# Chains of a Fourier filter and soft mixture of experts: two batches in one stationary operand, row steps behind the chain's copies, three weight loads under way

## The chip, the core and the metric

The kernel runs on one core of one Trainium2 chip. The metric is the device time of one execution in microseconds (us). The kernel has TensorE (PE; its weight loads are shown as PEld), VectorE (DVE), ScalarE (ACT), GpSimd (POOL), the SyncE queue (SP) that issues nearly all DMAs, and 16 DMA engines.

## What is computed

x has 8 batches of 2496 tokens and 256 features. Each feature is filtered along the tokens by a product in the frequency domain, and the result, as 19968 tokens, goes through a soft mixture of 8 experts with 4 slots each.

```python
X = np.fft.rfft(x, axis=1)
y = np.fft.irfft(X * (filt_r + 1j * filt_i)[None], n=2496, axis=1)
x = y.reshape(19968, 256)
logits = x @ phi                        # 32 slots
d = softmax(logits, axis=0)             # over all tokens: dispatch
slot_in = (d.T @ x).reshape(8, 4, 256)
slot_out[e] = relu(slot_in[e] @ w1[e]) @ w2[e]      # w1 256x1024, w2 1024x256
c = softmax(logits, axis=1)             # over the slots of each token: combine
out = c @ slot_out
```

All is float32; one matrix product of float32 is two loads and two passes on TensorE, a transposition one of each.

## The kernel before

2496 = 39 x 64, and the Fourier transform is done in two steps by matrix products. The first step (`s1_unit`, tile s) multiplies the 39-point part, its result `at` goes to DRAM (a_dram) and comes back turned (ash). `x_unit` does the 64-point part (tile x) and multiplies with the filter on DVE (tiles t, yt; from batch 6 on partly on POOL), in ten units of two rows for each batch. `t_unit` transposes the result (tile t on TensorE, y in SBUF) and makes logits in the frequency domain (tile l, lt). The filtered tokens themselves are never formed: the mixture works on y and on logits that a small inverse transform makes.

This second part is a chain for each group of batches: groups 0, 1 and 2 are pairs, (0,1), (2,3), (4,5), and groups 3 and 4 are the single batches 6 and 7. The chain (function `chain`, a generator) goes through transposed logits (ltr, copied to lsb by DVE), two steps of an inverse transform (v1 products into v_0, v_7 and v_14, by the first of their seven rows, copied by ACT; transposed; lg products), the running maximum (cm, cmax, mt, mx, mb, m_run), the exponential of the dispatch (d, by DVE and ACT), the forward transform of it (u products, copied to u by ACT; transposed and copied to u2 by DVE; dd products, copied by ACT), sums z and s with y, and then the row steps (`rows`) for the softmax over slots: maximum rm, difference and exponential in place in lg, sum r_all, reciprocal. For groups 0 and 1 the finished lg is written to DRAM (c_dram) and read back at the end (cl).

In the products v1 and u the stationary operand is 32 slots of one batch wide. A pair makes four products, which write the four strips of 32 partitions of PSUM, for batch and half. A single batch makes two.

The order of instructions on each engine comes from a scheduler that follows data dependences and the order of the program text; `behind` and `not_before` add a dependence of order alone, with no wait on a semaphore. In the program, each slot of the main loop (80 slots, ten for each batch) issues an x unit, one or two first steps, a t unit and two hops of the active chain, where a hop runs to the next `yield`. The last two chains are interleaved by the table `TAIL`, and there `in_line` makes TensorE keep the program's order. The expert weights, 64 blocks of 256 KB in the order `WORDER`, are loaded by SP into buffers as they come free (`load_w`, `load_ws`): the filter table ff_t, then ash, t2, yb, y and yt in the first 43, and y again for the rest, as s of the last batches releases them. A load waits for the buffer, and SP goes strictly in order. Then come the expert layers (h, ht, o, slot_out), and the combine with the output (ct, out, ob), which SP writes to DRAM.

## Time and profile before

| | |
|---|---|
| runs | 396.33, 396.37, 392.46 us; median 396.33 |
| profiled execution | 398.42 us, span of its instructions 396.6 us, mean granted TensorE clock 0.924 |
| TensorE busy | 359.1 us of products, 267.3 us of weight loads |
| DVE, ACT, POOL busy | 257.5, 177.0, 151.7 us |
| DMA | 103.99 MB, mean 262 GB/s |
| first output issued | 343.47 us from the span's start |

Times in the profile count from the span's start. Matrix products overlap, so their busy time isn't a rate; the rate of a run of products is read from its length in the chain of waits, divided by their number. The granted clock is the share of full speed at which TensorE ran. In the DMA view, queue q1 holds the kernel's own transfers, and the queues marked "instruction" bring instructions to the engines. What lies between the span and the execution's time is 1.8 us.

### The profile page before, as it was taken

The numbers are of one execution on the slowest core, as the hardware profiler recorded it, in microseconds if no ns is written. First come the engines' busy times: TensorE is split into PE (matmuls) and PEld (weight loads), VectorE is DVE, ScalarE is ACT, GpSimd is POOL, SyncE is SP. The second block draws the span as 40 slices with busy tenths as digits, with TensorE's granted clock in tenths as the row PEclk, the third lists the DMA queues.
The fourth block names the chain that finished last, engine by engine and source line by source line (L and its number), as shares of the span: only waits on it lengthen the run. The fifth ranks groups of instructions, "written<-read, shape, count | busy, mean of one in ns | idle before, by whom it ended". The sixth has DMA issues, their size and how long they took to land.

```text
span 396.6 us, 11597 instructions
## 1 busy us (share of the span) xinstructions
PE 359.1 (91%) x4778; PEld 267.3 (67%) x4778; DVE 257.5 (65%) x517; ACT 177.0 (45%) x357; POOL 151.7 (38%) x182
## 2 busy tenths in 40 slices
PE   8998798869998999999799999998988899999970
PEld 6985476647765766765576678787667544778970
DVE  1484767763899966589986555897553453586650
ACT  2554344525456533545734354463352431575540
POOL 0374645526545243255515284553221131361000
PEclk9999989987999999999989999999995999996555
DMA  8769999898889896868867576773488597299997
GB/s 316 257 213 301 289 272 311 287 333 241 283 279 322 240 285 209 264 196 267 251 206 224 170 208 187 271 215 106 135 266 319 193 250 252 114 415 415 417 417 294
DMA packets 50155, 103.99 MB, mean 262 GB/s; under 512 B 5218, under 2 KB 23394, under 8 KB 47926
## 3 DMA queue, kind: packets, MB, share of 16 engines
q1 hardware_dynamic: 49412, 102.83, 78.2%
q8 instruction: 38, 0.62, 0.6%
q10 hardware_dynamic: 690, 0.42, 0.4%
q14 instruction: 15, 0.12, 0.1%
HBM read 63.11 MB, written 40.12 MB: 260 GB/s over the span
## 4 chain that ended last, share of the span: by engine, by line
PE 72%; DVE 9%; DMA 9%; POOL 3%; issue 3%; ACT 2%; SPq 0%; POOLq 0%; DVEq 0%; ACTq 0%
PE x L423 14%; PE t L452 7%; PE out L1054 7%; PE s L355 7%; DMA xt<-in_x 5%; PE s L496 5%; PE l L470 4%; PE v L496 4%; DMA ash<-a_dram 3%; PE dd L496 3%; PE lg L496 3%; PE u L496 2%; PE s L396 2%; PE h L998 2%; PE o L1016 2%
## 5 line engine op out<-in xcount | busy, mean ns | idle before, releaser
L423 PE MATMUL x<-cst_t,ash 128*128 128x128 f32 x640 | 91.2, 285 | 5.3 <-DMA ash<-a_dram 2.9
L423 PEld LDWEIGHTS x<-cst_t,ash 128*128 128x128 f32 x640 | 81.3, 196 | 16.0 <-DVE t L440 5.3
L334 POOL TENSOR_TENSOR eo<-xt 128x512 f32<-128x512 f32 (+1 forms) x40 | 48.5, 1212 | 104.6 <-issue 61.0
L440 DVE TENSOR_TENSOR t<-x,ff_t 128x512 f32<-128x512 f32 x80 | 54.9, 686 | 49.6 <-PE x L423 33.0
L364 ACT COPY at<-s 128x1024 f32<-128x1024 f32 (+1 forms) x42 | 39.5, 941 | 58.0 <-PE s L355 37.8
L452 PE MATMUL t<-cst_t,yt 128*128 128x128 f32 x320 | 52.8, 285 | 0.0
L452 PEld LDWEIGHTS t<-cst_t,yt 128*128 128x128 f32 x320 | 37.0, 144 | 20.4 <-issue 11.1
L337 POOL TENSOR_TENSOR eo<-xt 128x512 f32<-128x512 f32 (+1 forms) x40 | 49.6, 1239 | 0.0
L355 PE MATMUL s<-eo,w1q_t 64*64 64x512 f32 (+1 forms) x336 | 43.9, 593 | 5.4 <-POOL eo L337 5.4
L460 ACT COPY y<-t 128x512 f32<-128x512 f32 x58 | 33.5, 589 | 21.1 <-PE t L452 18.1
L442 DVE TENSOR_TENSOR x<-x,ff_t 128x512 f32<-128x512 f32 x60 | 41.6, 695 | 1.3
L1054 PE MATMUL out<-so,st 32*128 32x256 f32 x468 | 35.9, 367 | 1.0 <-DVE ob L1059 0.8
L1054 PEld LDWEIGHTS out<-so,st 32*128 32x128 f32 x468 | 32.8, 252 | 3.4 <-DVE ob L1059 1.4
L1059 DVE COPY ob<-out 128x512 f32<-128x512 f32 (+1 forms) x40 | 25.2, 670 | 8.4 <-PE out L1054 7.5
L443 DVE TENSOR_TENSOR yt<-x,t 128x256 f32<-128x256 f32 x60 | 25.1, 418 | 7.7 <-PE l L470 6.4
L470 PE MATMUL l<-yt,phi_t 128*32 128x128 f32 x640 | 27.5, 286 | 2.6 <-ACT y L460 2.0
L1059 ACT COPY ob<-out 128x512 f32<-128x512 f32 (+1 forms) x40 | 21.9, 581 | 14.0 <-PE out L1054 11.5
L443 POOL TENSOR_TENSOR yt<-yt,t 128x256 f32<-128x256 f32 x20 | 15.0, 750 | 33.1 <-DVE yt L442 33.1
L470 PEld LDWEIGHTS l<-yt,phi_t 128*32 128x32 f32 x640 | 16.0, 111 | 13.8 <-issue 7.5
L480 ACT COPY lt<-l 128x128 f32<-128x128 f32 x40 | 10.6, 266 | 33.0 <-PE l L470 32.8
L444 DVE TENSOR_TENSOR yt<-x,t 128x256 f32<-128x256 f32 x60 | 24.7, 412 | 0.0
L496 PE MATMUL u<-cst_t,d 117*32 117x60 f32 (+1 forms) x704 | 15.3, 219 | 5.3 <-ACT u L634 2.7
(116 smaller groups left out, 505.1 us busy)
## 6 DMA issues: line engine op xcount, KB each, us to landing
xt<-in_x SPq DMA_DIRECT2D x35, 512.0 KB, 5.6
ash<-a_dram SPq DMA_DIRECT2D x70, 256.0 KB, 4.0
out<-ob SPq DMA_DIRECT2D x17, 1024.0 KB, 8.0
a_dram<-at SPq DMA_DIRECT2D x56, 240.0 KB, 4.6
w<-in_wx SPq DMA_DIRECT2D x32, 256.0 KB, 4.1
w<-in_wx SPq DMA_DIRECT2D x6, 512.0 KB, 5.1
x_t<-in_x SPq DMA_DIRECT2D x5, 512.0 KB, 5.5
ff_t<-in_ff SPq DMA_DIRECT2D x10, 256.0 KB, 5.4
```

What stands on the lines that cost most here:

```text
L334: ins = eng.tensor_tensor(out=eo[:, 0, 0:n], in0=xs[:, :, 0], in1=xs[:, :, 1], op=ALU.add)
L337: ins = eng.tensor_tensor(out=eo[:, 1, 0:n], in0=xs[:, :, 0], in1=xs[:, :, 1], op=ALU.subtract)
L355: ins = pe.matmul(ps, w1q_t[q, c], eo[q, c, 0:n], start=True, stop=True)
L423: ins = pe.matmul(ps[:, 2 * k + dh].rearrange("q r c -> q (r c)"), ash[:, k, dh * P : (dh + 1) * P], C("a1" if t0 + k else "b0"), start=Tr ...
L440: dve.tensor_tensor(out=t2, in0=ps[:, :, ::-1, :], in1=fiv, op=ALU.mult)
L442: dve.tensor_tensor(out=part, in0=ps, in1=frv, op=ALU.mult)
L443: add.tensor_tensor(out=yt[:, :, 1, :], in0=part[:, :, 1, :], in1=t2[:, :, 1, :], op=ALU.add)
L452: pe.transpose(pt[:, k, dh, :], yt[:, c % 2, 2 * k + dh].rearrange("q r c -> q (r c)"), ident)
L470: ins = pe.matmul(pl[32 * j : 32 * j + 32, :], phi_t[:, dh, :], yt[:, j // 2, 2 * (j % 2) + dh].rearrange("q r c -> q (r c)"), start=(dh = ...
L496: line(pe.matmul(*a, **k))
L1054: nc.tensor.matmul(prs[k][:, mm, :], sts[n][q, hs, c0 : c0 + P], so[q, ho], start=(i == 0), stop=(i == 2))
L1059: copy(ob[:, nm * k : nm * (k + 1), :], prs[k])
```

## The change

- Pairs: lsb, d, u2, dd, lg and cl are laid out with the two batches of a pair side by side, so that one product takes 64 columns (both batches) as its stationary operand. v1 and u make two products where there were four. For single batches (M = 32) nothing changes.
- Row steps: in groups 0 to 2 the first row step on DVE (maximum) is ordered behind the last copy of u2 on DVE, and the exponentials on ACT behind the last copy of dd on ACT. This is an order of issue, not a wait on a semaphore.
- Weight loads: for the loads from ash to yt (`calm`), each load waits until the load three places before it in the program has landed. The loads before and after it have no such wait.

```diff
--- before.py
+++ after.py
@@ -72,6 +72,7 @@
 WL = 4
 SB = 3
 AT_ONCE = 1
+UNDER_WAY = 3


 def slot_of(b, u):
@@ -509,16 +510,17 @@

         nb = len(bs)
         R = nb * 64
-        lsb = wk.tile([P, nb, NT, SLOTS], F32, tag="cc", name=f"lsb_{g}", bufs=1)
+        M = nb * SLOTS
+        lsb = wk.tile([P, NT, nb, SLOTS], F32, tag="cc", name=f"lsb_{g}", bufs=1)

         def ltr(b2, i0):
             b = bs[b2]
-            lf = lsb[:, b2].rearrange("k t e -> k (t e)")
             pl = psum([P, 4, P], f"ltr_{b}_{i0}")
             n = min(4, 5 - i0)
             for i in range(n):
                 pe_t(pl[:, i, :], lts[b][:, i0 + i, :], ident)
-            dve.tensor_copy(lf[:, i0 * P : (i0 + n) * P], pl.rearrange("k i q -> k (i q)")[:, 0 : n * P])
+            lf = pl.rearrange("k i (j e) -> k (i j) e", j=4)
+            dve.tensor_copy(lsb[:, 4 * i0 : 4 * (i0 + n), b2], lf[:, 0 : 4 * n])

         for b2 in range(nb):
             for i0 in (0, 4) if nb == 2 else (0,):
@@ -532,22 +534,20 @@
             n = min(7, NT - t0)
             pv = psum([P, 7, KP // 2, 2], f"v1_{g}_{t0}")
             for t in range(t0, t0 + n):
-                for b2 in range(nb):
-                    for h in range(2):
-                        q = (b2 * 2 + h) * 32
-                        pe_m(
-                            pv[q : q + 32, t - t0].rearrange("q k r -> q (k r)"),
-                            lsb[:, b2, t, :],
-                            C("m1" if t else "m0", h * KP, (h + 1) * KP),
-                            start=True,
-                            stop=True,
-                        )
+                for h in range(2):
+                    pe_m(
+                        pv[M * h : M * h + M, t - t0].rearrange("q k r -> q (k r)"),
+                        lsb[:, t].rearrange("k b e -> k (b e)"),
+                        C("m1" if t else "m0", h * KP, (h + 1) * KP),
+                        start=True,
+                        stop=True,
+                    )
             act.copy(v1[0:R, :, :, t0 : t0 + n], pv[0:R, 0:n].rearrange("q t k r -> q k r t"))
             yield f"v1_{t0}"
         v = wk.tile([QP, NH, R], F32, tag="cb", name=f"v_{g}", bufs=1)
-        lg_t = lgp.tile([KR, NH, nb, 2, SLOTS], F32, tag=f"lg{max(g, NSPILL)}", name=f"lg_{g}")
+        lg_t = lgp.tile([KR, NH, 2, nb, SLOTS], F32, tag=f"lg{max(g, NSPILL)}", name=f"lg_{g}")
         lgs[g] = lg_t
-        lg = lg_t.rearrange("s a b h e -> s a (b h e)")
+        lg = lg_t.rearrange("s a h b e -> s a (h b e)")
         cm = wk.tile([KR, 3, SLOTS], F32, tag="cm", name=f"cm_{g}", bufs=1)
         v1f = v1.rearrange("q k r t -> q (k r t)")
         SA = 512 // R
...
@@ -592,7 +592,7 @@
         else:
             dve.tensor_copy(m_new, pmb)
         d = wk.tile([KR, NX, SLOTS], F32, tag="cb", name=f"d_{g}", bufs=1)
-        dv = d.rearrange("s (a b h) e -> s a b h e", b=nb, h=2)
+        dv = d.rearrange("s (a h b) e -> s a h (b e)", b=nb, h=2)
         HT = NT // 2
         u = wk.tile([P, HT, 2 * N2], F32, tag="ca", name=f"u_{g}", bufs=1)
         mbc = m_new[0:KR].rearrange("s (o e) -> s o e", o=1)
@@ -618,38 +618,37 @@
                     i = h * NH + a
                     kr, jn = (KR, PK) if i < NI - 1 else (N1, 1)
                     r0 = (a - a0) * 2 * PK
-                    for b2 in range(nb):
-                        for th in range(2):
-                            q = (b2 * 2 + th) * 32
-                            pe_m(
-                                pu[q : q + 32, h, r0 : r0 + 2 * jn].rearrange("q r t -> q (r t)"),
-                                dv[0:kr, a, b2, h, :],
-                                C("w1d", th * PK * NT, th * PK * NT + jn * NT)[0:kr],
-                                start=True,
-                                stop=True,
-                            )
+                    for th in range(2):
+                        pe_m(
+                            pu[M * th : M * th + M, h, r0 : r0 + 2 * jn].rearrange("q r t -> q (r t)"),
+                            dv[0:kr, a, h],
+                            C("w1d", th * PK * NT, th * PK * NT + jn * NT)[0:kr],
+                            start=True,
+                            stop=True,
+                        )
             for h in range(2):
                 k0 = (h * NH + a0) * PK * 2
                 nk = min((h * NH + a0 + n) * PK, N2) * 2 - k0
                 act.copy(u[0:R, :, k0 : k0 + nk], pu[0:R, h, 0:nk].rearrange("q r t -> q t r"))
             yield f"u{a0}"
         TG = SA if nb == 2 else HT // 2
-        u2 = wk.tile([P, HT, nb, 2, SLOTS], F32, tag="cc", name=f"u2_{g}", bufs=1)
-        dd = wk.tile([P, HT, nb, 2, SLOTS], F32, tag="cb", name=f"dd_{g}", bufs=1)
+        ended = [None, None]
+        u2 = wk.tile([P, HT, 2, nb, SLOTS], F32, tag="cc", name=f"u2_{g}", bufs=1)
+        dd = wk.tile([P, HT, 2, nb, SLOTS], F32, tag="cb", name=f"dd_{g}", bufs=1)
         for t0 in range(0, HT, TG):
             n = min(TG, HT - t0)
             pu = psum([P, TG, R], f"u2_{g}_{t0}")
             for t in range(n):
                 pe_t(pu[:, t, :], u[0:R, t0 + t, :], ident[0:R, 0:R])
-            dve.tensor_copy(u2[:, t0 : t0 + n].rearrange("k t b h e -> k t (b h e)"), pu[:, 0:n])
+            ended[1] = dve.tensor_copy(u2[:, t0 : t0 + n].rearrange("k t h b e -> k t (h b e)"), pu[:, 0:n])
             yield f"u2_{t0}"
         for t0 in range(0, HT, TG):
             n = min(TG, HT - t0)
-            pd = psum([P, TG, nb, 2, SLOTS], f"dd_{g}_{t0}")
+            pd = psum([P, TG, 2, nb, SLOTS], f"dd_{g}_{t0}")
             pe_m(pd[:, 0:n], C("b1"), u2[:, t0 : t0 + n], start=True, stop=True)
             if t0 == 0:
-                pe_m(pd[:, 0, :, 0, :], C("bh"), u2[:, 0, :, 0, :], start=True, stop=True)
-            act.copy(dd[:, t0 : t0 + n], pd[:, 0:n])
+                pe_m(pd[:, 0, 0], C("bh"), u2[:, 0, 0], start=True, stop=True)
+            ended[0] = act.copy(dd[:, t0 : t0 + n], pd[:, 0:n])
             if t0 != 0:
                 yield "dd"

...
@@ -703,16 +702,20 @@
                 ins = dve.tensor_reduce(out=rm[:, sl], in_=lgf[:, sl], axis=AX.X, op=ALU.max)
                 if x0 == 0 and "sit" in queue:
                     behind("sit", ins)
+                if not late:
+                    not_before(ins, ended[1])
                 rmb = rm[:, sl].rearrange("s (x o) -> s x o", o=1).broadcast_to([KR, step, SLOTS])
                 dve.tensor_tensor(out=lgf[:, sl], in0=lgf[:, sl], in1=rmb, op=ALU.subtract)
-                act.activation(lgf[:, sl], lgf[:, sl], AF.Exp)
+                ins = act.activation(lgf[:, sl], lgf[:, sl], AF.Exp)
+                if not late:
+                    not_before(ins, ended[0])
                 yield "rows"
                 dve.tensor_reduce(out=rs[:, sl], in_=lgf[:, sl], axis=AX.X, op=ALU.add)
                 yield "rows"
             dve.tensor_scalar(out=rs, in0=rs, scalar1=1e-9, scalar2=None, op0=ALU.add)
             dve.reciprocal(out=rs, in_=rs)
             if g < NSPILL:
-                c_dram[g] = scr.tile([KR, NH, nb, 2, SLOTS], F32, name=f"c_dram{g}", bufs=1)
+                c_dram[g] = scr.tile([KR, NH, 2, nb, SLOTS], F32, name=f"c_dram{g}", bufs=1)
                 for lo, hi in ((0, CR), (CR, KR)):
                     sp.dma_start(c_dram[g][lo:hi], lg_t[lo:hi])

@@ -839,12 +842,18 @@
                 hop(len(active) - 1)

     wt = {}
+    w_ins = []
+    calm = [False]

     def load_w(t, n):

         n = min(n, len(WORDER) - len(wt))
         lo = len(wt)
-        sp.dma_start(t[:, 0 : 512 * n].rearrange("q (n f) -> q n f", f=512), wx[:, lo : lo + n])
+        ins = sp.dma_start(t[:, 0 : 512 * n].rearrange("q (n f) -> q n f", f=512), wx[:, lo : lo + n])
+        if calm[0] and len(w_ins) >= UNDER_WAY:
+            info = mybir.DependencyInfo(mybir.DependencyClass.Sync, mybir.DependencyReason.DATA)
+            tc.add_manual_dep(ins.ins, w_ins[-UNDER_WAY].ins.name, info, reason="transfers under way")
+        w_ins.append(ins)
         for k in range(n):
             wt[WORDER[lo + k]] = t[:, k * 512 : (k + 1) * 512]

@@ -896,6 +905,7 @@
                 for _ in range(3):
                     next(final)
         hop_slot(n)
+    calm[0] = True
     load_ws(prod, "ash", ASH, bufs=ASH)
     load_ws(prod, "t2", 2)
     k = NS % YB - CPB
@@ -903,6 +913,7 @@
         load_w(big[0][:, c].rearrange("q k d -> q (k d)"), 1)
     load_ws(ypool, "y", YB - 3 * CPB + k)
     load_ws(prod, "yt", 2, 2)
+    calm[0] = False
     while active[0][0] < NG - 2:
         hop()
     run(NG - 2, "d")
...
@@ -946,11 +957,11 @@
         g, b2 = where[b]
         nb = len(GROUPS[g])
         cl = lgs[g]
-        rv = r_all[:, g, 0 : 2 * nb * NH].rearrange("s (a b h) -> s a b h", b=nb, h=2)
+        rv = r_all[:, g, 0 : 2 * nb * NH].rearrange("s (a h b) -> s a h b", b=nb, h=2)
         c1 = tail.tile([KR, 2, NH, SLOTS], F32, tag="c1", name=f"c1_{b}")
         for h in range(2):
-            rb = rv[:, :, b2, h : h + 1].broadcast_to([KR, NH, SLOTS])
-            nc.gpsimd.tensor_tensor(out=c1[:, h], in0=cl[:, :, b2, h], in1=rb, op=ALU.mult)
+            rb = rv[:, :, h, b2 : b2 + 1].broadcast_to([KR, NH, SLOTS])
+            nc.gpsimd.tensor_tensor(out=c1[:, h], in0=cl[:, :, h, b2], in1=rb, op=ALU.mult)
         cq = tail.tile([KR, 2, 4, SLOTS], F32, tag="cr", name=f"cr_{b}")
         nc.gpsimd.tensor_copy(cq[:, 0, 0:3], c1[:, 0, 8:11])
         nc.gpsimd.tensor_copy(cq[:, 0, 3:4], c1[:, 1, 8:9])
```

The order of instructions on three engines shows what the scheduler makes of it. First ACT, around the dispatch of group 1: d is the dispatch's exponential, lg the row steps' exponential, u the copies that TensorE's u products wait for. Before:

```order
L604 ACTIVATE d_2346<-d_2346 117x512
L604 ACTIVATE d_2346<-d_2346 117x384
L665 ACTIVATE al_2646<-al_2646 128x32
L480 COPY lt_2196<-l_4_2693 128x128
L708 ACTIVATE lg_2234<-lg_2234 117x704 x2
L364 COPY at_4_2737<-s_6_4_2732 128x1024
L634 COPY u_2347<-u_0_2379 128x10x24 x2
L634 COPY u_2347<-u_4_2416 128x10x24 x2
L634 COPY u_2347<-u_8_2488 128x10x18
L634 COPY u_2347<-u_8_2488 128x10x14
```

Now, from the last copies of u on (dd are the chain's copies further on):

```order
L632 COPY u_2223<-u_8_2332 128x10x18
L632 COPY u_2223<-u_8_2332 128x10x14
L365 COPY at_5_2653<-s_6_5_2648 128x1024
L461 COPY yb_4_2251<-t_2_2659 128x512
L461 COPY yb_4_2251<-t_3_2691 128x512
L365 COPY at_0_2687<-s_7_0_2682 128x512
L481 COPY lt_2615<-l_1_2697 128x128
L651 COPY dd_2348<-dd_0_2431 128x512
L365 COPY at_1_2756<-s_7_1_2751 128x1024
L651 COPY dd_2348<-dd_4_2435 128x512
L651 COPY dd_2348<-dd_8_2438 128x256
L709 ACTIVATE lg_2110<-lg_2110 117x704 x2
```

The two exponentials of lg stood between the dispatch and the copies of u; now they stand behind the last copy of dd.

TensorE, where u of group 2 meets v of group 3 (a single batch). Before:

```order
L493 MATMUL ltr_4_3818<-cst_t,lt_3201 128x128
L423 MATMUL x_5_3835<-cst_t,ash_5_3588 128x128 x4
L496 MATMUL u_0_3379<-cst_t,d_3349 32x60 x32
L496 MATMUL u_4_3416<-cst_t,d_3349 32x60 x32
L496 MATMUL u_8_3482<-cst_t,d_3349 32x60 x20
L496 MATMUL u_8_3482<-cst_t,d_3349 32x20 x4
L496 MATMUL v_3_14_3821<-cst_t,lsb_3686 32x66 x12
L452 MATMUL t_3_3845<-cst_t,yt_2_3701 128x128
L470 MATMUL l_1_3852<-yt_2_3701,phi_t 32x128 x8
```

Now:

```order
L494 MATMUL ltr_4_3566<-cst_t,lt_3005 128x128
L424 MATMUL x_5_3583<-cst_t,ash_5_3336 128x128
L497 MATMUL u_0_3171<-cst_t,d_3141 64x60 x16
L497 MATMUL u_4_3192<-cst_t,d_3141 64x60 x16
L497 MATMUL v_3_14_3569<-cst_t,lsb_3434 32x66 x6
L497 MATMUL u_8_3242<-cst_t,d_3141 64x60 x10
L497 MATMUL u_8_3242<-cst_t,d_3141 64x20 x2
L497 MATMUL v_3_14_3569<-cst_t,lsb_3434 32x66 x6
L424 MATMUL x_5_3583<-cst_t,ash_5_3336 128x128 x3
L453 MATMUL t_3_3593<-cst_t,yt_2_3449 128x128
L471 MATMUL l_1_3600<-yt_2_3449,phi_t 32x128 x8
```

The u products of the pair are half as many with outputs of 64 partitions, and the last part of v (v_14) stands partly ahead of u_8; the v products of the single batch are as they were.

SP, the weight loads around the end of the main loop; ff_t with 128x1024 is a double load, ash and t2 are shown as w. Before:

```order
L847 DMA ff_t<-in_wx 128x1024
L306 DMA ash_9_3794<-a_dram_2849 128x512
L847 DMA w_4060<-in_wx 128x512
L847 DMA ff_t<-in_wx 128x1024
L847 DMA w_4062<-in_wx 128x512
L847 DMA w_4064<-in_wx 128x512
L847 DMA ff_t<-in_wx 128x1024
L847 DMA w_4066<-in_wx 128x512
L847 DMA w_4068<-in_wx 128x512
L847 DMA ff_t<-in_wx 128x1024
L847 DMA yb_8_3991<-in_wx 128x512
L847 DMA w_4070<-in_wx 128x512
```

Now:

```order
L307 DMA ash_9_3542<-a_dram_2681 128x512
L852 DMA ff_t<-in_wx 128x1024
L852 DMA w_3808<-in_wx 128x512
L852 DMA ff_t<-in_wx 128x1024
L852 DMA w_3810<-in_wx 128x512
L852 DMA ff_t<-in_wx 128x1024
L852 DMA w_3812<-in_wx 128x512
L852 DMA w_3814<-in_wx 128x512
L852 DMA w_3816<-in_wx 128x512
L852 DMA w_3818<-in_wx 128x512
L852 DMA w_3820<-in_wx 128x512
L852 DMA yb_8_3739<-in_wx 128x512 x8
```

The double loads of ff_t now stand ahead of three of the ash loads, and both t2 loads ahead of the eight of yb.

## The prediction

> **What bounds the kernel now.** I read the page first, then the chain of waits, windows over the last third, the DMA view of single stretches, and the timeline of two places. The last two rows of this first piece are of the timeline and of the windows table (us, then busy us and instruction count of PE, PEld, DVE, ACT, POOL; granted clock, DMA share, GB/s).

> ```profile
> PE 359.1 (91%) x4778; PEld 267.3 (67%) x4778; DVE 257.5 (65%) x517; ACT 177.0 (45%) x357; POOL 151.7 (38%) x182
> q8 instruction: 38, 0.62, 0.6%
> PE 72%; DVE 9%; DMA 9%; POOL 3%; issue 3%; ACT 2%; SPq 0%; POOLq 0%; DVEq 0%; ACTq 0%
> 343.47 42.80 SPq L1073 DMA_DIRECT2D out<-ob  x22
> 350.00:360.00 10.00, 9.20 (x131) 7.58 (x130) 8.58 (x18) 6.74 (x17) 5.32 (x15) 1.00 1.01 413
> ```

> TensorE carries 72% of the chain, up to the first output at 343.5 us. From there the DMA engines are full (share 1.01, 413 GB/s) and about 53 us follow whatever TensorE does. So a gain counts only if it brings the first output forward. In the tail, the chain of waits (start, us, what) has one hole:

> ```profile
> 291.67 0.44 PE t L452 x4
> 293.48 1.57 PE v L496 x54
> 296.05 2.00 issue
> 298.05 0.51 PE u L496 x12
> ```

> "issue" means that no semaphore explains the wait. Windows around it:

> ```profile
> 291.60:298.04 6.44, 4.45 (x130) 3.96 (x129) 2.46 (x8) 3.91 (x11) 0.00 (x0) 1.00 1.03 356
> 298.00:300.00 2.00, 1.95 (x47) 1.95 (x48) 0.00 (x0) 0.85 (x3) 0.00 (x0) 0.65 1.05 404
> 300.00:308.00 8.00, 7.43 (x49) 5.58 (x45) 3.06 (x7) 1.32 (x4) 1.54 (x2) 0.50 0.72 268
> 308.00:310.00 2.00, 1.76 (x19) 0.87 (x23) 0.76 (x3) 1.07 (x3) 0.00 (x0) 0.79 0.00 0
> 271.09:298.04 26.95, 24.95 (x378) 19.51 (x379) 14.55 (x35) 10.71 (x26) 5.61 (x8) 1.00 0.58 182
> 166.90:271.09 104.19, 98.84 (x1510) 74.66 (x1510) 81.60 (x150) 50.29 (x98) 51.53 (x54) 0.98 0.72 217
> ```

> After the hole the clock stands at 0.65, 0.50 and 0.79: lost are 2 x 0.35 + 8 x 0.50 + 2 x 0.21 = 5.1 us of TensorE time. I read the hole as TensorE running out of instructions. Queue 8 makes 38 transfers, and 2 x 4778 instructions over 38 is 251 each. Two more "issue" holes lie on the chain:

> ```profile
> 162.88 0.94 PE v L496 x56
> 166.32 0.59 issue
> 269.84 1.26 issue
> ```

> From the end of the first to the end of the second run 2 x 1510 = 12 x 252 instructions, from there to the third 378 + 379 = 3 x 252: each hole is at a block boundary. Where a block is short instructions, TensorE finishes it before the next arrives. The DMA view of 291.7 to 295.7 and of 295.7 to 296.9 (queue, packets, MB, share):

> ```profile
> q1 hardware_dynamic: 743, 1.35, 102.0%
> q1 hardware_dynamic: 241, 0.44, 100.5%
> q8 instruction: 1, 0.02, 5.2%
> ```

> The block is entered at 291.6, yet the refill starts after 295.7, behind weight loads that fill every engine, and TensorE resumes at 298.05. [...]

> **The operand of 64 columns.** For the three pairs it halves 40 v and 44 u sets of passes: 252 matrix products fewer, each two loads and two passes, so 1008 instructions or four blocks. A set, 4 instructions, takes 0.94/14 = 67 ns for v. A single batch makes a set of two instructions, 1.57/27 = 58 ns (row at 293.48). For u:

> ```profile
> 193.66 1.89 PE L496 MATMUL u<-cst_t,d 117*32 117x60 f32 x128
> 314.52 0.70 PE u L496 x24
> ```

> Here it is 1.89/32 = 59 against 0.70/12 = 58 ns. So TensorE saves 9 ns x 40 x 3 = 1.1 us. No row shows two 64-column halves fed from 128 rows. If they ran one after the other, a set would cost two half-width passes. That is excluded by the first step, whose 64-column products share the array:

> ```profile
> 161.16 1.02 PE s L355 x8
> 278.99 0.86 PE lg L496 x2
> ```

> Eight products of 512 columns take 1.02 us there, where at 0.43 us each (lg) they would take 3.4. Weight loads of 64 columns may still cost up to 2 us in all by the overlap not being perfect; I take a gain of 0.5, since about half of the chain before 288 waits on others. The holes at 166 and 269 lie in pair bursts that are now half as many instructions: 0.59 + 1.26 = 1.85 us, of which I take 1.5. [...]

> **The row steps.** Now they stand in the middle of the dispatch:

> ```profile
> 193.68 2.22 DVE L707 TENSOR_TENSOR lg<-lg,rm 117x704 f32<-117x704 f32 x2
> 195.99 0.79 ACT L708 ACTIVATE lg<-lg 117x704 f32<-117x704 f32 x1 [0.55 <-DVE lg L707]
> 197.58 1.15 ACT L634 COPY u<-u 128x240 f32<-128x240 f32 x4
> 198.26 0.92 PE L496 MATMUL u<-cst_t,d 117*32 117x60 f32 x48 [2.71 <-ACT u L634]
> 129.15 0.64 PE L470 MATMUL l<-yt,phi_t 128*32 128x128 f32 x16 [2.01 <-ACT y L460]
> 198.00:204.00 6.00, 5.41 (x74) 5.05 (x75) 5.08 (x12) 2.39 (x7) 0.00 (x0) 0.72 0.84 224
> 100.00:150.00 50.00, 47.99 (x651) 33.83 (x649) 44.49 (x86) 25.27 (x47) 22.49 (x18) 1.00 0.89 284
> ```

> ScalarE's copy of u stands behind two exponentials, which wait for DVE; TensorE waits 2.71 us, and in group 0 2.01 us. The clock then falls once (0.72 over 6 us, 1.7 us lost). Moving the row steps behind the copies of u2 and dd takes this away: at most 6.4 us. But DVE is busy 44.5 of 50 us there and keeps all its work, so the next x units wait instead; the spill to DRAM moves later on SP, too, with stores of the first step and x loads behind it. Bounds: a loss of 1 to a gain of 6.4. I take 1.0, near the low end, because DVE and DMA (0.89) are nearly full. In group 2 the steps move to a stretch that is now 277 to 288 us, with the maximum mx of group 3 behind them on DVE:

> ```profile
> 283.59 2.83 PE s L496 x49
> 283.97 0.26 DVE L586 TENSOR_REDUCE mx<-mt 32x1 f32<-32x117 f32 x1
> ```

> The products s of group 2 cover that; without this cover 0.26 us of mx would show. Before the tail: 0.5 + 1.5 + 1.0 = 3.0 us.

> **Three loads under way.** At the boundary near 291.6 the SP queue now issues the last double load of ff_t, and the first held load waits for its landing. So when the refill is asked for, some 0.5 MB are under way instead of 1.3. The hole goes if the refill is 2.0 us earlier. I take it that it does: gain 2.0 plus 4.9 of the 5.1 us of clock (the chain has some copies there), 6.9 us. What is late next are the weights:

> ```profile
> w<-in_wx SPq DMA_DIRECT2D x32, 256.0 KB, 4.1
> w<-in_wx SPq DMA_DIRECT2D x1, 256.0 KB, 2.6
> yb<-in_wx SPq DMA_DIRECT2D x8, 256.0 KB, 6.6
> DMA packets 3086, 6.49 MB, mean 278 GB/s; under 512 B 355, under 2 KB 355, under 8 KB 3081
> 332.97 0.33 SPq L847 DMA_DIRECT2D w<-in_wx  x1
> 334.39 5.32 PE o L1016 x96
> ```

> The first row is the page's median of all single loads. A load alone lands in 2.6 us, with many under way in 6.6. Behind a held load SP has only further weight loads, the reads of the spilled groups and the outputs. With three I take 2.9: 0.79 MB per 2.9 us is 271 GB/s. From about 292 on, 6.0 MB are held so (19 single and 2 double loads): 22 us, and SP is through at about 311. The rest, 6.5 MB (fourth row, of 310.2 to 333.5), took 23 us, part of it waiting for buffers; I take 20 to 22. The last weight lands at 331 to 333 and is needed by the last 32 instructions of o, from 338 - 6.9 = 331 on. So some 2.4 us are given back: 4.5 us remain. Bounds: 6.9 gained, or a loss (second rival).

> Sum: the profiled execution took 398.42 us, its span 396.6 and 1.8 around it. 398.4 - 3.0 - 4.5 = 390.9. Its median run is 2.1 us faster, so it may hold less of these stalls; 396.3 - 7.5 would be 388.8. I say 390.

> **Rivals.** First: the refill stays late. It is one transfer among hundreds, and at 269 it came late with little traffic. If its wait isn't set by the backlog, the limit does nothing for it, the hole and the half clock stay, and only the 3.0 us before the tail remain, less what chance does to the clock: 393 to 396. For it speaks the hole at 269.84; against it the four full microseconds without the refill. [...]

> Second, slower: the held loads are too slow. If a load with two others takes the 4.1 us of the page's median, the rate is 192 GB/s, 6.0 MB take 31 us, SP is through at 321 and the last weight lands at 341 to 343. Then o waits 3 to 5 us past its old time, against which stand 3.0 us: 396 to 402, with a cold clock on top. It decides at a landing of about 3.5 us. Against it: three loads alone use only 2 us of the engines' time (0.79 MB at the 404 GB/s of the row 298:300).

> Third: DVE has room after all, and the gains before the tail come in full: 1.1 + 1.85 + 6.4 + 4.5 = 13.9 us less, 382 to 385.

> **The numbers.** Forecast (387 to 393) 0.52; refill still late 0.25; slow weights 0.15; the large gain 0.08. What the measurement can tell from no change is 1%, 4 us. Faster than 392.4: 0.08, most of the forecast (0.46) and 0.04 of the first rival, 0.58. Slower than 400.3: 0.10, of the second rival with a cold clock. Range 385.5 to 398, which leaves out the large gain and the worse half of the second rival.

> **What would show it.** TensorE instructions fall to 2 x 4274. The hole in u of group 3 (now at 296.05) is gone and the granted clock stays 1.0 until 340: right; the hole there with weights at a lower rate: the first rival. The wait of u or l for ScalarE beside the exponentials of the rows is gone in groups 0 and 1, and something of DVE stands in the chain 10 us later. If h or o waits for a weight DMA, the second rival is at work. I am wrong if the first output is issued later than 340 us.

## The result and the profile after

Over 20 runs of each kernel, before took 394.84 us (391.68 to 398.36) and after 391.72 us (390.19 to 394.42). The ratio is 0.994, with a 95% interval of 0.9915 to 0.9965: a gain of 1.4 to 3.4 us (3.1 by the medians), where 6.3 were forecast. The profiled executions took 398.42 and 394.42 us. Their stages, in us from the span's start:

| | before | after | moved |
|---|---|---|---|
| u of group 3 starts | 292.0 | 282.6 | -9.4 |
| h starts | 322.8 | 307.3 | -15.5 |
| o starts | 331.9 | 316.4 | -15.5 |
| o ends | 339.7 | 335.6 | -4.1 |
| first output issued | 343.5 | 339.4 | -4.1 |
| end of the span | 396.6 | 392.5 | -4.1 |

The chain gained far more than forecast, and nearly three quarters of that were given back inside o. The rows of the page of after that answer to those of before (busy us and count of each engine; queue 8: transfers, MB, share; the chain by engine and by line):

```profile
PE 357.7 (91%) x4274; PEld 264.5 (67%) x4274; DVE 256.8 (65%) x517; ACT 176.1 (45%) x357; POOL 151.0 (38%) x182
q8 instruction: 34, 0.56, 0.6%
PE 74%; DMA 14%; DVE 3%; ACT 2%; issue 2%; SPq 1%; POOL 1%; DVEq 0%; ACTq 0%; POOLq 0%
```

TensorE has the 504 fewer products and 504 fewer loads, and queue 8 four transfers fewer. Its busy time fell by only 1.4 us. DMA's share of the chain has grown from 9% to 14%. Where, the chain of waits of after shows, from h to the expert outputs (start, us, what):

```profile
307.34 3.64 PE h L1009 x32
...
310.99 6.87 DMA w<-in_wx
...
317.93 10.03 DMA w<-in_wx
...
328.00 3.94 PE o L1027 x20
...
335.62 1.22 PE slot_out L1038 x4
```

A weight load issued at 317.93 releases o at 328.0. In before, the last 96 passes of o ran through in 5.32 us. In after o takes 19.2 us instead of 7.8. Windows of after over that place, in the columns of the prediction's windows:

```profile
316.00:322.00 6.00, 6.00 (x90) 3.25 (x88) 1.81 (x3) 0.60 (x1) 0.00 (x0) 1.00 1.03 291
322.00:328.00 6.00, 0.04 (x2) 0.00 (x1) 0.00 (x0) 0.00 (x0) 2.41 (x6) 0.68 0.97 255
328.00:334.00 6.00, 5.94 (x35) 2.21 (x36) 0.00 (x0) 0.00 (x0) 0.00 (x0) 0.75 0.86 306
```

TensorE stands still for 6 us. Two us into that the clock falls to half for 6.8 us (from 324.1 to 330.9), and behind it the weights go on coming one by one: from 315 to 340 us the weight loads (PEld) of o waited for DMA in eight places (us in total, times, longest):

```profile
PEld o L1027 <- DMA w<-in_wx: 9.4, 8, 6.4
```

Both stretch the rest of o. The DMA engines are full meanwhile. Ahead of it, everything is as hoped. TensorE over groups 0 to 2 (120 to 282 us: busy us and count, clock, DMA share, GB/s), first before, then after:

```profile
120.00:282.00 162.00, 154.05 (x2353) 115.32 (x2350) 125.06 (x237) 76.61 (x148) 73.25 (x74) 0.99 0.74 224
```

```profile
120.00:282.00 162.00, 160.75 (x2070) 120.14 (x2069) 127.57 (x246) 78.31 (x155) 74.21 (x78) 1.00 0.73 222
```

TensorE was idle for 162 - 154.05 = 7.95 us there, and now for 1.25. In u of group 3 the hole is gone and the clock stays at 1.0.

### The profile page after: what moved, and what is told of

The parts are those of the page before. It is cut to its first block, busy times and chain, and to the rows that moved or that the text cites. A ratio compares the mean times of both kernels' runs of the same rounds, so it can differ in the third digit from the quotient of the medians.

```text
span 392.5 us, 10594 instructions
## 1 busy us (share of the span) xinstructions
PE 357.7 (91%) x4274; PEld 264.5 (67%) x4274; DVE 256.8 (65%) x517; ACT 176.1 (45%) x357; POOL 151.0 (38%) x182
## 4 chain that ended last, share of the span: by engine, by line
PE 74%; DMA 14%; DVE 3%; ACT 2%; issue 2%; SPq 1%; POOL 1%; DVEq 0%; ACTq 0%; POOLq 0%
PE x L424 17%; PE t L453 8%; PE s L356 8%; PE out L1065 7%; DMA w<-in_wx 6%; PE s L497 5%; PE l L471 5%; DMA ash<-a_dram 4%; PE u L497 3%; PE v L497 3%; PE s L397 3%; PE dd L497 3%; PE lg L497 3%; PE o L1027 2%; DMA xt<-in_x 2%
## 5 line engine op out<-in xcount | busy, mean ns | idle before, releaser
L424 PE MATMUL x<-cst_t,ash 128*128 128x128 f32 x640 | 89.1, 281 | 6.7 <-DMA ash<-a_dram 3.5
L424 PEld LDWEIGHTS x<-cst_t,ash 128*128 128x128 f32 x640 | 79.3, 193 | 15.3 <-issue 4.5
L335 POOL TENSOR_TENSOR eo<-xt 128x512 f32<-128x512 f32 (+1 forms) x40 | 48.1, 1202 | 99.5 <-issue 56.0
L453 PE MATMUL t<-cst_t,yt 128*128 128x128 f32 x320 | 51.4, 281 | 0.0
L338 POOL TENSOR_TENSOR eo<-xt 128x512 f32<-128x512 f32 (+1 forms) x40 | 48.5, 1212 | 0.0
L356 PE MATMUL s<-eo,w1q_t 64*64 64x512 f32 (+1 forms) x336 | 42.8, 580 | 4.9 <-POOL eo L338 4.9
L497 PE MATMUL s<-y,dd 128*32 128x256 f32 x232 | 19.9, 381 | 0.4 <-ACT dd L651 0.3
## 6 DMA issues: line engine op xcount, KB each, us to landing
ash<-a_dram SPq DMA_DIRECT2D x70, 256.0 KB, 3.8
w<-in_wx SPq DMA_DIRECT2D x32, 256.0 KB, 4.7
ff_t<-in_ff SPq DMA_DIRECT2D x10, 256.0 KB
```

The lines of the kernel that those rows point to most:

```text
L335: ins = eng.tensor_tensor(out=eo[:, 0, 0:n], in0=xs[:, :, 0], in1=xs[:, :, 1], op=ALU.add)
L338: ins = eng.tensor_tensor(out=eo[:, 1, 0:n], in0=xs[:, :, 0], in1=xs[:, :, 1], op=ALU.subtract)
L356: ins = pe.matmul(ps, w1q_t[q, c], eo[q, c, 0:n], start=True, stop=True)
L424: ins = pe.matmul(ps[:, 2 * k + dh].rearrange("q r c -> q (r c)"), ash[:, k, dh * P : (dh + 1) * P], C("a1" if t0 + k else "b0"), start=Tr ...
L453: pe.transpose(pt[:, k, dh, :], yt[:, c % 2, 2 * k + dh].rearrange("q r c -> q (r c)"), ident)
L497: line(pe.matmul(*a, **k))
```

## The experiments

Each kernel was timed beside before on the same chip.

**No limit on the loads** (`a_nolimit`). The change with its limit out of reach:

```diff
-UNDER_WAY = 3
+UNDER_WAY = 99
```

> The changed kernel without the limit on weight loads (eight under way, as before). Theory W (the late weights eat what the chain gained): the weights land about 6 us earlier, o waits 3 us or less instead of some 15, and the first output is issued at 335 us or before unless the hole in u of group 3 comes back; 387 to 390 us if it doesn't, 390 to 392 if it does. Rival H (the limit is what closes the hole, and the hole is dear): the hole of 2 us and a clock of 0.5 behind it return, and the time is 393 to 396 us.

Measured: 385.13 us against 394.59, ratio 0.9717 (0.9655 to 0.9778). By the medians the limit costs 391.7 - 385.1 = 6.6 us, and the rest of the change gains 9.5; by the ratios (0.994 and 0.9717) the limit costs 8.8 us. The two were timed at different times, so this is rough. The hole came back, as a row of TensorE's timeline shows (start, us, line and tiles, in brackets the idle time before):

```profile
290.80 0.61 PE L497 MATMUL u<-cst_t,d 117*32 117x60 f32 x16 [1.55 <-issue]
```

The DMA view of the same kernel from 284.2 to 288.2 and from 288.2 to 289.3, and then that of after from 283.0 to 284.1 (its block of instructions is entered at 281.5):

```profile
q1 hardware_dynamic: 702, 1.50, 100.4%
...
q1 hardware_dynamic: 226, 0.42, 100.8%
q8 instruction: 1, 0.02, 5.4%
```

```profile
q1 hardware_dynamic: 10, 0.02, 13.7%
q8 instruction: 1, 0.02, 5.3%
```

Without the limit the engines are full and the block's refill comes 4.1 us after the block is entered. With it they are nearly idle and it comes after 1.5 us. So the limit does what it was said to, at a price in o. A second kernel without the limit, `f_nolimit_cl` below, has the same hole, of 1.65 us.

**The operand alone** (`b_merge`): the 64-column operand, without the limit and without the row steps' order.

```diff
 if not late:
-    not_before(ins, ended[1])
...
-UNDER_WAY = 3
+UNDER_WAY = 99
```

> Of the change only the operand of 64 columns: the row steps stand where they stood, and there is no limit. Theory W: the holes at 166 and 269 us go, the waits beside the row steps stay, h starts 2 to 5 us earlier and the time falls by 1 to 3 us, to 392 to 394. Rival (the array time of the products decides, and that is the same): no change, 394 to 396. The third hole in u of group 3 stays in both, since its place in the blocks of instructions is the same.

Measured: 385.73 us, 0.9774 (0.9725 to 0.9822), 6 to 8 us better than expected, and level with the whole change without its limit. What TensorE waited for from 120 to 282 us (us in total, times, longest):

```profile
PE l L471 <- ACT y L461: 1.4, 1, 1.4
```

No "issue" is among the waits, and of the two waits behind the row steps' exponentials only the one in group 0 is left, shorter (1.4 for 2.01 us). The one of 2.71 us at 195 is gone though no edit moved the row steps. The scheduler did: with the new operand it puts a copy of u between the two exponentials of group 1, as ScalarE's timeline of b_merge shows,

```profile
197.19 0.61 ACT L632 COPY u<-u 128x240 f32<-128x240 f32 x2
197.68 0.80 ACT L707 ACTIVATE lg<-lg 117x704 f32<-117x704 f32 x1
```

and on TensorE it splits the burst of u, where before ran 128 passes in a row. So this edit is half as many instructions and another order at once. TensorE is idle for 2.9 us of the 162 instead of 7.95.

The third hole, in u of group 3, was expected to stay here and did not. Its block was entered at 285.7 us and the refill began 1.8 us later; from 283 to 286 us the DMA share was 0.39, where a_nolimit had 0.97. So in this kernel the hole is gone without a limit.

**The row steps' order alone** (`c_rows`), put into before:

```diff
+                if not late:
+                    not_before(ins, ended[1])
...
-                act.activation(lgf[:, sl], lgf[:, sl], AF.Exp)
+                ins = act.activation(lgf[:, sl], lgf[:, sl], AF.Exp)
+                if not late:
+                    not_before(ins, ended[0])
```

> Of the change only the order of the row steps, with four products for a pair and no limit. Theory W: the waits of TensorE at 127 and 195 us go, and h starts 4 to 7 us earlier, since DVE has room after all; the holes at 166 and 269 stay; 390 to 393 us. Rival (DVE and the DMAs are full, what is moved is paid later, as the prediction had it): h starts 1 us earlier, 393.5 to 395 us.

Measured over 12 runs: 395.81 us, 1.0011 (0.9963 to 1.006), no gain. In the profiled execution, one of the fastest (392.08 us), h starts 6.3 us earlier; but 4.7 of that come behind the start of u of group 3, where the hole was 1.1 us instead of 2.0 and no half clock followed, and this edit changes nothing there. The waits for ScalarE at 127 and 195 are gone. In their place stands, in the chain of waits of c_rows in group 0:

```profile
123.67 1.50 PE u L496 x105
125.17 3.73 issue
128.90 0.25 PE u L496 x7
```

and, in its table of what TensorE waited for from 120 to 300 us:

```profile
PE u L496 <- issue: 4.8, 2, 3.7
PE x L423 <- DVE yt L444: 1.8, 1, 1.8
```

TensorE now runs through the burst of u without a stop for ScalarE, and reaches the end of its block before the next one has come. It is idle for 7.89 us of the 162, as in before. Of the rest, 1.8 us are a wait for DVE at 209 us, and 1.1 us an "issue" of x at 144.8 us, which is of another kind (see the part on the prediction).

**Moving the block boundaries** (`s_shift`): `c_rows` with 128 instructions ahead of everything.

```diff
 keep_warm(WM)
+keep_warm(32, 32)
```

> The kernel of the row steps' order alone, with 32 small warm-up products more at its start, 128 instructions: all later block boundaries of 256 instructions move by half a block in the program. Theory I (TensorE runs out of instructions where a whole block lies in a burst of short ones): the hole of 3.7 us in u of group 0 (at 125 us) and those in v of groups 1 and 3 (at 167 and 268) go; a boundary pair now encloses u of group 1 and u of group 2, so holes of 0.5 to 4 us come in the last part of u (u_8) of groups 1 and 2, near 195 and 265 us. Rival (the holes belong to the products or to their data): they stay where they were, at the same products.

One execution took 411.37 us. The 32 products made the warm-up 13.5 us longer (17.27 for 3.78), and the kernel late with it, so the time says nothing. The holes do (chain of waits of s_shift, groups 0 and 1):

```profile
114.62 0.81 PE v L496 x43
115.42 2.58 issue
...
210.14 2.63 PE u L496 x172
212.77 3.13 issue
```

The hole in u of group 0 and those in v at 167 and 268 are gone. A new one stands in u of group 1, as expected, and one in v of group 0. The one expected in u of group 2 did not come: its block ran through in 1.8 us, but the next refill had begun at 285.0 us, 0.7 us before TensorE started on it (285.7). With the same data, the same products and the same queues, holes move with the block boundaries: TensorE runs out of instructions. A count bears this out. The holes in v and u of before begin behind 3777, 6849 and 7617 recorded instructions of TensorE (its waits on semaphores included), those of c_rows behind 2753, 3777, 6849 and 7617, and the two of s_shift behind 1985 and 4801: all are whole multiples of 256 apart, to the instruction, though s_shift has 128 more ahead.

**The same shift with the new operand** (`h_merge_shift`): `b_merge` with that line.

> Only the 64-column operand, with 32 small warm-up products (128 instructions of TensorE) ahead, so that every block of 256 instructions begins elsewhere, as in s_shift. The warm-up products delay all by some 15 us (they did so in s_shift), so the time is not compared, only the holes. Theory (with half the instructions a pair's burst of v or u cannot hold a whole block, so a block lasts longer than a refill takes, wherever its boundary falls): no hole named issue of over 0.3 us in groups 0 to 2, whatever may stand in the bursts of the single batches. Rival (in the kernel with the operand alone the boundaries only happened to fall well): one to three such holes of 0.5 to 4 us in groups 0 to 2, as in s_shift, where the boundaries were moved in the same way with the old operand.

Its one execution took 405.5 us; only the holes are compared. What TensorE waited for from 115 to 312 us:

```profile
PE l L471 <- ACT y L461: 1.4, 1, 1.4
PE u L497 <- issue: 1.3, 1, 1.3
```

The only "issue" is at 308.2 us, in group 3, whose bursts the change leaves as they were. None stands in groups 0 to 2, so it is not luck of the boundaries. TensorE's instructions counted off in blocks of 256 say why. Without its idle time, the shortest block of groups 0 to 2 ran for 2.4 us in before and 1.8 in s_shift, against 5.7 in after, 6.0 in b_merge and 6.6 here (worked out from the times of every 256th instruction).

**The limit alone** (`d_limit`), put into before:

```diff
+        if calm[0] and len(w_ins) >= UNDER_WAY:
+            info = mybir.DependencyInfo(mybir.DependencyClass.Sync, mybir.DependencyReason.DATA)
+            tc.add_manual_dep(ins.ins, w_ins[-UNDER_WAY].ins.name, info, reason="transfers under way")
```

> Of the change only the limit on weight loads. Theory W: the hole in u of group 3 goes (the refill starts less than 2.2 us after its block is entered), h starts about 6 us earlier, and o waits for weights 3 to 6 us; the time changes by less than 2 us, 393 to 396. Rival (the hole isn't the refill behind weight loads): the hole stays, weights are late as well, 396 to 400 us.

Measured: 400.95 us, 1.012 (1.0053 to 1.0186), slower by 0.5 to 1.9%, and above both expected times. Its chain of waits:

```profile
327.78 9.35 DMA w<-in_wx
...
337.52 5.08 DMA w<-in_wx
...
342.64 1.05 PE o L1025 x10
```

h starts at 317.5, 5.3 us earlier than before, since the hole and the half clock are gone; yet o ends at 343.7, 4.0 later. The hole went as expected, but o lost 9.3 us, where waits of 3 to 6 were expected. Here the second rival stands as it was written.

**What makes the weights late.** Three kernels change one thing each: the reads of the spilled groups (cl) behind the last weight, with the limit (`e_cl`) and without (`f_nolimit_cl`), and five loads under way (`g_five`).

```diff
-sp.dma_start(lgs[g][lo:hi], c_dram[g][lo:hi])
+not_before(sp.dma_start(lgs[g][lo:hi], c_dram[g][lo:hi]), w_ins[-1])
```

> The changed kernel with its limit of three, and the reads of the spilled groups behind the last weight load. Theory W: the 1.3 MB ahead of the last eleven weight loads take 4 to 5 us that o waits for; the wait of o shrinks by that, and the time falls to 386.5 to 389 us. Rival (o's weights come late because the held loads are slow and the buffers come free late, not for the reads): 390 to 392 us. Combine for the fourth output batch could wait for cl instead.

> The changed kernel without the limit, and the reads of the spilled groups (cl, 1.3 MB) ordered behind the last weight load on SP. Theory W: if o still waits for weights without the limit (its last product ends 8.1 us after its first, where 128 products at the pace of before take 7.8), the reads cost nothing there and nothing is gained: 384 to 386.5 us. Rival (the reads stand in the way of weights that somebody waits for): 2 to 4 us less, 381 to 383 us.

> The changed kernel with five loads under way in place of three. Theory W: the rate of the held loads goes from some 215 to 300 GB/s or more and SP is through about 6 us earlier; o hardly waits; the hole in u of group 3 is short or gone; 384 to 386.5 us, level with no limit at all. Rival H (the limit closes the hole only when it is strict): 386.5 to 390 us with the hole back.

Measured: e_cl 386.6 us, 0.9827 (0.9783 to 0.9871); f_nolimit_cl 385.15, 0.979 (0.9738 to 0.9841); g_five 384.02, 0.9784 (0.9732 to 0.9836). So the four reads of 1.3 MB in all cost some 5 us where the limit is, and nothing where it isn't. The DMA views say how: first after from 316 to 328 us, which begins with the reads, then e_cl from 307 to 316, which has only weights:

```profile
DMA packets 1364, 3.28 MB, mean 273 GB/s; under 512 B 174, under 2 KB 174, under 8 KB 1364
```

```profile
DMA packets 1615, 3.24 MB, mean 360 GB/s; under 512 B 180, under 2 KB 180, under 8 KB 1615
```

The engines are full in both (share 1.03 and 0.97 in the windows of after above, 1.01 for queue q1 in e_cl), but with the reads they move a quarter less. With five under way a hole of 0.57 us is left in u of group 3 and o waits for nothing.

**The order on SP** (`k_own`). SP's timeline of after shows another thing (start, us, queue, line, DMA and count):

```profile
271.03 0.33 SPq L852 DMA_DIRECT2D ff_t<-in_wx  x1
274.54 0.33 SPq L852 DMA_DIRECT2D w<-in_wx  x1
279.48 0.33 SPq L852 DMA_DIRECT2D ff_t<-in_wx  x1
282.98 5.07 SPq L852 DMA_DIRECT2D w<-in_wx  x5
288.40 10.63 SPq L852 DMA_DIRECT2D yb<-in_wx  x8
299.20 15.78 SPq L852 DMA_DIRECT2D w<-in_wx  x18
315.31 2.22 SPq L939 DMA_DIRECT2D cl<-c_dram  x4
317.93 10.15 SPq L852 DMA_DIRECT2D w<-in_wx  x8
328.13 0.90 SPq L852 DMA_DIRECT2D yb<-in_wx  x2
329.65 0.33 SPq L852 DMA_DIRECT2D w<-in_wx  x1
```

The first three held loads (the first is at 267.47) each go 3.5 to 3.6 us behind a double load of ff_t: in the program the last three ff_t loads are the ones "three before", and they come only as the main loop frees ff_t. All other loads stand behind them. From 250 to 282 us the DMA share is 0.43, against 0.61 in before. At 283 us 42 weight loads are left, where the kernel without a limit had 37. `k_own` counts only held loads:

```diff
-        w_ins.append(ins)
+        if calm[0]:
+            w_ins.append(ins)
```

> The whole change, but a held load waits only for the held load three places before it, not for the double loads of ff_t. In the changed kernel the first three held loads (ash) are issued at 267.47, 274.54 and 282.98 us, each 3.5 us behind a double load of ff_t, since that is one of the three before them; SP then has 42 weight loads left at 283 us, where the kernel without a limit has 37. Theory O (the order that the limit forces on SP is part of what makes the weights late): 37 or 38 loads left at 283 us, the last weight is issued 4 to 6 us earlier (324 to 326 us instead of 329.65), o waits for weights 2 us at most in one place, 386 to 388.5 us, ratio 0.978 to 0.985. Rival R (only the rate of three loads under way and the reads of the spilled groups count): the last weight issued at 328 us or later, o still waits 4 us or more, 390 to 392 us. A hole in u of group 3 may come back in part under O, 0 to 1.5 us, since one double load of ff_t falls beside held loads there.

Measured: 387.56 us against 394.08, 0.9827 (0.9774 to 0.988), no hole, and SP's timeline of k_own ends

```profile
324.65 0.37 SPq L852 DMA_DIRECT2D w<-in_wx  x1
```

5.0 us earlier than in after. o ends at 330.7 instead of 335.6, still slowed by several waits of about 1 us or less. SP has 35 loads left at 283 us, where 37 or 38 were expected. So Theory O holds; that the reads and the rate account for what remains is not shown by a run of its own.

**Putting them together** (`i_merge_five_cl`, `j_five_cl`): five loads under way and cl last, without the row steps' order and with it.

> The 64-column operand without the row steps' order, five loads under way, the reads of the spilled groups behind the last weight. Theory: the row steps' order is worth what remains of the one wait for ScalarE in group 0, 0 to 1.5 us, once the operand is changed; so this and j_five_cl lie within 1.5 us of each other, both 383 to 386 us, ratio 0.97 to 0.978. Rival: the row steps' order carries part of the gain: this one is 2 us or more slower than j_five_cl.

> All of the change with five loads under way instead of three, and the reads of the spilled groups behind the last weight. If the two cures of the late weights add up: 382 to 384 us, ratio 0.968 to 0.975, with o waiting for no weight and no hole over 0.6 us in u of group 3. If with five the reads are no longer in the way: 384 to 385.5, the same as with five alone.

Measured: 385.58 us, 0.977 (0.9722 to 0.9819), without the order; 383.51 us, 0.9719 (0.9674 to 0.9764), with it. The intervals overlap and the profiled spans are 381.6 and 381.2 us: whether the order is worth the 2 us between the medians isn't settled. j_five_cl beats both before and after. In its chain o runs without a wait, from 316.5 to 324.3 us:

```profile
318.97 5.32 PE o L1027 x96
```

Its interval does not part it from a_nolimit (0.9717) or g_five (0.9784).

## Why the prediction was wrong in size

The direction was right, and the time lies in the range. That is in part luck: of the three terms of the sum two were mis-sized, in opposite directions. The one that made the gain fall short is the last, the weights. In the profiled execution the sum was -3.0 - 6.9 + 2.4 = -7.5, and measured were -9.4 - 6.1 + 11.4 = -4.1.

**Before the tail, 3.0 us forecast, 9.4 measured.** The step that failed here is the discount: 1.0 out of 6.4 for the row steps, "because DVE and DMA (0.89) are nearly full". They were busy, but TensorE hardly waited for them: after the change its waits over 0.5 us from 120 to 282 us are down to one of 1.1 us. That one is the wait for DVE that was forecast. It is called "issue", but no instruction transfer runs from 138 to 144 us. DVE's timeline and then TensorE's have

```profile
139.99 1.52 DVE L708 TENSOR_TENSOR lg<-lg,rm 117x704 f32<-117x704 f32 x1
...
142.50 0.41 DVE L445 TENSOR_TENSOR yt<-x,t 128x256 f32<-128x256 f32 x1
```

```profile
143.01 0.46 PE L424 MATMUL x<-cst_t,ash 128*128 128x128 f32 x2 [1.07 <-issue]
```

A row step holds up the products of the x unit on DVE, and x goes on 0.1 us after the last of them. This stop of 1.0 to 1.1 us stands in all nine kernels that have the row steps' order and in none of the five that don't. So in after the order has a price on DVE of about 1 us, and not of 5.4.

The upper bounds, 1.85 for the two holes, 6.4 for the two waits and the clock, and 1.1 for the operand, are 9.35 together, the third rival's sum up to the tail. That the total agrees is luck in part. Of the 9.4 us, 1.4 are there at the start of u of group 0 already (125.7 us before, 124.2 after); before had 6.8 us of half clock from 87.0 us on and after 3.4 from 88.6, each at the end of a wait for GpSimd (of 3.2 us to 87.6, and of 3.0 to 87.3), and no part of the change explains that. The hole at 269.84 also isn't in a pair's burst, as the prediction has it: the passes there are v of group 3, a single batch, behind 176 passes of the pair's u, most of them in the same block. The 2 us that the loads of 64 columns might have cost are in no row, and the 1.1 us of array time isn't there either: the chain of waits of after has for the pairs

```profile
93.23 0.97 PE v L497 x28
...
124.29 1.54 PE u L497 x46
...
192.02 1.66 PE u L497 x52
```

which are 69 ns for a set of two passes (0.97/14) and 64 to 67 (1.66/26, 1.54/23), where four passes took 67 and 59. Sets of 64 columns run no faster. The worth of the operand lies in half as many instructions and in the order that the scheduler makes of them; the runs don't part the two. And b_merge shows that it takes away the wait at 195 by itself, while c_rows shows that the row steps' order without it only trades waits for a hole. I had added the two edits up as if they were independent.

**The hole, 6.9 us forecast, 6.1 measured** (from the start of u of group 3 to that of h): right in mechanism and size. The first rival ("the limit does nothing for it") is refuted by after against a_nolimit and f_nolimit_cl, with g_five between them, and by d_limit against before. The limit is not the only way, though: b_merge has no hole without it.

**The weights, 2.4 us given back forecast, 11.4 measured.** This is the step that cost the forecast its gain, and it is the second rival's mechanism. It did not lead to a slower kernel only because the gain ahead of it was 15.5 us. "SP is through at about 311", counted from 292, is 19 us; it took 24.4 (282.98 to 307.35), of which 17 loads at 1.2 us each (282.98 to 303.39), 218 GB/s instead of 271. The rest was to take 20 to 22 us until the last landing. The last load was only issued after 22.3, and o ended 28 us behind SP's getting through. Two causes I had in view but did not price: the order on SP, quoted before the prediction (the ff_t loads ahead of three ash loads), which k_own shows to be worth 4 to 5 us (o ends 4.9 us earlier, the median is 4.2 lower), and the reads of the spilled groups, which I counted by their bytes and which e_cl shows to be worth 5.

**What was to show it:** 4274 instructions, the hole gone, the waits beside the exponentials gone, o waiting for a weight DMA, and the first output before 340 us all came as written. "Something of DVE in the chain 10 us later" came some 15 us behind the wait that went, as the stop of 1.1 us at 142 us, under the name "issue".

In u of group 3 the refill began 4.2 us after its block was entered in before (291.61 to 295.79) and 4.1 us in a_nolimit, both with the engines full, and 1.5 us in after, with three loads under way (281.49 to 283.02). A short wait can still leave a hole, as at 269.84 in before: the refill began 1.3 us after the block was entered (267.32 to 268.67), with queue q1 at 32% (268.0 to 269.84), and TensorE had run through the block in 2.5 us.

## What to carry to other kernels

- A run of short products can stall on the fetch of its own instructions (2.00 us in u of group 3 of before): look for "issue" holes in bursts, whole blocks of 256 instructions apart (behind 3777, 6849 and 7617 in before). The name alone doesn't say it: the stop at 142 us was a wait for DVE, of 1.1 us. Fewer, wider instructions cured it here (b_merge has no "issue" among its waits from 120 to 282 us); an edit that only lets the burst run through may bring it on (3.73 us in u of group 0 of c_rows).
- A limit on transfers under way is also an order on the queue (k_own, which counts only held loads, issued the last weight 5.0 us earlier). Count which loads each one waits for in the program, and what stands behind it, before pricing its rate.
- Where a later stage has a supply of its own, price the supply's end as a time, not as a correction to the gain: a gain upstream of 6 us more than forecast was worth nothing here until the weights came earlier.
- A change of one operand's shape lets the scheduler order the program anew. Read the order on each engine before putting the gain down to the operand.

## What the hardware showed

```profile
118.00:130.00 12.00, 11.99 (x108) 1.00 0.69 220
```

against those of h_merge_shift

```profile
311.40:314.80 3.40, 3.35 (x12) 0.51 1.05 398
```

  Up to the outputs the drops of before last 3.4, 6.8, 3.4 and 10.2 us, those of after 3.4 and 6.8. The length of a hole was a poor guide to whether it cost clock: in before, the wait of 2.01 us that ended at 129.15 brought no drop, the hole of 2.00 us that ended at 298.05 the one of 10.2.
- Three loads of 256 KB under way moved 218 GB/s, with 1.2 us for each (after, 282.98 to 303.39). That is about half of the 404 to 413 GB/s that full engines moved in before (298 to 300 and 350 to 360 us).
